# Weight parts laid out by use, three preparation buffers and a rewritten order in a fused convolution and SwiGLU kernel

## The chip, the cores and the metric

The kernel runs on one core of one Trainium2 chip. The metric is the device time of one execution in microseconds (us), as a median of several runs. Engines are named as in the profile: PE is TensorE's matmuls and PEld its weight loads, DVE is VectorE, ACT is ScalarE, POOL is GpSimd, SP is SyncE, which here issues almost all DMAs.

## What is computed

The input x has 8 sequences of 4096 tokens with 192 features. A causal convolution with 7 taps per head (8 heads of 24 features, taps through a softmax) is followed by a feed-forward block: RMS norm, a gate and a value product of 192 to 1536, SiLU, and an output product back to 192. All of it is in fp32.

```python
def _attn_ref(x, weight):
    w = np.exp(weight - np.max(weight, axis=-1, keepdims=True))
    w = w / (np.sum(w, axis=-1, keepdims=True) + 1e-09)
    ...
    out = np.einsum('hk,bskhg->bshg', w, x_unf)

def _moe_ref(x, w_gate, w_val, w_out, rms_g):
    rms = np.sqrt(np.mean(x * x, axis=-1, keepdims=True) + 1e-06)
    xn = x / rms * rms_g
    g = xn @ w_gate
    silu = g * (1.0 / (1.0 + np.exp(-g)))
    val = xn @ w_val
    return (silu * val @ w_out).astype(np.float32)
```

## The kernel before

**Tiles and pairs.** Tokens are taken in 32 pairs of 1024 (`PAIRS`), each two halves of 512. The first pair is computed with plain fp32 products (`plain`, `outer`). The second pair's gate and value products are plain too (line 871), while its output product already uses seven products instead of eight per block. From the third pair on all is in Strassen-Winograd form: sums of token halves (`x_sum`, line 827, words x1 to x4) meet sums of weight blocks, and each fp32 operand is split into three parts of the matmul format fp32r: a rounded high part (word n, line 667 or 669), a low part (word l, line 813) and a remainder (word d, line 815), in `split`. There are five token operands 0 to 4; operands 0, 1 and 2 are the tokens as they were fetched, 3 and 4 are the sums.

**Weight preparation.** During the second pair's products the ten weight operands (`NW`) are prepared, each by `prepare(o)` in six steps: an optional difference on POOL (line 749), the high part on DVE (752) with a scaled copy on ACT (756), the low part on DVE (758), a difference on POOL (762), the last part on ACT (764) and a store to DRAM (768). The parts lie in one of two buffers (`o % 2`) in the tile `part1`. The 1536 hidden features are six column blocks j; `FORM` says which of them use operands 2, 4, 6 and 8 (blocks 1, 2, 4, 5) and which use operand 9 (blocks 0 and 3). `blocks(o)` gives a slice of blocks to prepare: for the four blocks 1, 2, 4, 5, which are not evenly spaced, it gives all six.

**The ring.** The stored parts come back through `ring_load` (line 785) into ten slots, in the order in which TensorE uses them; a slot is loaded again when its last use is done. The first ten loads are issued by `ring_start`. The ring's tile takes the place of `lent`, in which the third pair's tokens lie (`tokens(2)`), so it can be loaded only when these have been read.

**Order.** Nothing is scheduled: every engine executes its instructions in the order written down in four tables. `LINE` holds the 110 words of TensorE for a pair: 68 product words of six matmuls (such as P1.1 or Q4.1: product name and block; A, B and E words belong to the blocks of form 0), and 42 output words (o1.0: output product 1, block 0). `ORDER` holds the words of the other engines for one pair, each with its engine ahead (V for DVE, A for ACT, G for POOL, S for SP); `p3` means that TensorE's line goes on by three words, and a trailing `+` or `-` that the word belongs to the next or the previous pair. `FIRST` is the same for the second pair, where `W` is the next step of the weight preparation and `R` is `ring_start`. `PLAIN` is the order of the second pair's 24 product cells: for each block the four cells a, b, c, d, of two halves each.

The other words: `ga` to `gd` is the SiLU of a cell on ACT (line 976), `ma` to `md` the product with the value half on DVE (line 983), which frees the cell's PSUM buffer (there are four); `f1`, `f3` copies and `f4`, `f5` sums (line 970) that complete cells in PSUM; `h1` to `h4` the sums of hidden blocks for the output products (line 953); `c1`, `s7`, `c2`, C22, C21 copies and sums of output accumulators, T11 to T22 the transposes of the output (line 941). For the pairs to come: `cv0` to `cv6` the taps (cv0 on ACT, line 433, the others on DVE, line 437), `sq`, `red`, `pow`, `bc`, `mul` the norm, `pl` the store of the normed tokens to a DRAM scratch, `ft` their fetch back in transposed form (line 638), `ld` the load of x (line 146), `st` the store of the output.

The second pair therefore ends so: its 24 cells, then its 42 output words, among which stand the third pair's sums and splits, in `ORDER`'s first rows; `R` stands at the end of `FIRST`, but takes effect when the last of these splits has read the tokens.

Of the kernel before, what the change touches and what calls it, by code (L numbers as in the profile page):

```python
# [20 lines left out]
def kernel(  # L21
# [11 lines left out]
    P = nc.NUM_PARTITIONS  # L33
# [24 lines left out]
    PAIRS = B * NB  # L58
# [13 lines left out]
    PLAIN = tuple((j, c) for j in range(NP) for c in "abcd")  # L72
    ORDER = (
# [28 lines left out]
    )  # L102
    LINE = (
# [615 lines left out]
    def blocks(o):  # L719

        kind = {2: 1, 4: 1, 6: 1, 8: 1, 9: 0}.get(o)
        mine = [j for j in range(NP) if kind in (None, FORM[j])]
        step = {b - a for a, b in zip(mine, mine[1:])}
        if len(step) > 1:
            return slice(0, NP)
# [557 lines left out]
```

## Time and profile before

| | us |
|---|---|
| median of 3 runs (2518.46 to 2523.32) | 2521.33 |
| the profiled execution | 2519.95 |
| its span, first to last instruction | 2518.1 |
| mean granted TensorE clock | 0.996 of full speed |

Of the rows below, those of a group read: line, engine, operation, tile written and tiles read, shape, count, then busy time, mean ns of one, and the engine's idle time ahead of them with what ended it. Rows of a timeline read: start, length, engine, line, operation; in brackets the engine's idle time just before and what ended it. Rows of windows read: from and to, length, busy us and count of PE, PEld, DVE, ACT and POOL, granted clock, busy share of the DMA engines, GB/s.

### The profile page before, as it was taken

What the parts mean: (1) busy time and instruction counts of PE and PEld (TensorE: products, weight loads), DVE (VectorE), ACT (ScalarE), POOL (GpSimd) and SP (SyncE); (2) the same over time, 40 slices, a digit from 0 to 9 for tenths busy, and PEclk for the clock granted to TensorE, in tenths of its full rate; (3) what the DMA queues carried; (4) which work ended last, traced back from release to release, by engine and by line L of the source; (5) the groups of instructions that cost most, each with busy time, mean ns of one, the idle gap of its engine ahead of it and who ended that gap; (6) DMA issues with size and microseconds to landing.
All of it is one profiled execution on the core that took longest, in us unless ns stands there. A gap on an engine that the chain in (4) does not pass through costs nothing.

```text
span 2518.1 us, 69213 instructions
## 1 busy us (share of the span) xinstructions
PE 2479.5 (98%) x29152; PEld 1919.2 (76%) x29152; DVE 2102.1 (83%) x2642; ACT 999.8 (40%) x1405; POOL 653.5 (26%) x538
## 2 busy tenths in 40 slices
PE   8988999999999999999999999999999999999998
PEld 5535777877777777878777778777777887777776
DVE  8676888898888898888898888898888898888874
ACT  6342443333443433443433443433443433443432
POOL 0551323122322122322122322122322122222222
PEclk9998999999999999999999999999999999999999
DMA  7272776666776666776666776666876666766653
GB/s 149 59 222 65 194 201 179 162 173 168 196 201 176 165 170 166 201 200 174 162 171 167 206 194 179 160 169 171 206 190 179 161 168 175 206 187 178 162 153 100
DMA packets 717415, 432.12 MB, mean 172 GB/s; under 512 B 510330, under 2 KB 703410, under 8 KB 717106
## 3 DMA queue, kind: packets, MB, share of 16 engines
q1 hardware_dynamic: 713360, 426.78, 65.0%
q8 instruction: 230, 3.77, 0.6%
q10 hardware_dynamic: 3746, 0.92, 0.2%
q14 instruction: 79, 0.65, 0.1%
HBM read 366.96 MB, written 60.56 MB: 170 GB/s over the span
## 4 chain that ended last, share of the span: by engine, by line
PE 92%; DVE 2%; DMA 1%; SPq 1%; issue 1%; POOL 1%; ACT 1%; DVEq 0%; POOLq 0%; ACTq 0%
PE ps L899 57%; PE ps L926 34%; PE ps L871 1%; DMA wd<-part 1%; SPq L230 0%; SPq L146 0%; POOL part L762 0%; DVE y L437 0%; DVE ht L1098 0%; DMA hs<-in_moe_w_out_dram 0%; DVE part L758 0%; DVE part L815 0%; DVE part L813 0%; DMA x<-in_x_dram 0%; DMA ht<-in_moe_w_gate_dram 0%
## 5 line engine op out<-in xcount | busy, mean ns | idle before, releaser
L899 PE MATMUL ps<-part,ring 64*128 64x512 f32 x12240 | 1447.6, 392 | 4.2
L899 PEld LDWEIGHTS ps<-part,ring 64*128 64x128 f32 x12240 | 1174.2, 184 | 264.2 <-issue 34.7
L976 ACT ACTIVATE tt<-ps 128x512 f32<-128x512 f32 x744 | 442.1, 599 | 1017.8 <-PE ps L899 939.4
L983 DVE TENSOR_TENSOR ht<-ps,tt 128x512 f32<-128x512 f32 x744 | 500.2, 686 | 211.6 <-ACT tt L976 204.3
L926 PE MATMUL ps<-ht,wo_sb 128*32 128x384 f32 (+2 forms) x7272 | 458.2, 380 | 12.8 <-DVE ht L953 12.0
L953 POOL TENSOR_TENSOR ht<-ht 128x512 f32<-128x512 f32 x152 | 209.2, 1386 | 898.9 <-PE ps L926 565.3
L926 PE MATMUL ps<-ht,x 128*32 128x384 f32 (+2 forms) x6696 | 419.5, 379 | 0.0
L926 PEld LDWEIGHTS ps<-ht,wo_sb 128*32 128x32 f32 x7272 | 322.9, 110 | 122.7 <-issue 23.3
L437 DVE SCALAR_TENSOR_TENSOR y<-xh,tp,y 128x1536 f32<-128x1536 f32 x186 | 349.2, 1877 | 13.7 <-ACT y L433 12.5
L926 PEld LDWEIGHTS ps<-ht,x 128*32 128x32 f32 x6696 | 294.8, 110 | 86.3
L970 DVE TENSOR_TENSOR ps<-ps,tt 128x1024 f32<-128x1024 f32 x240 | 295.6, 1232 | 57.7 <-PE ps L899 29.5
L667 ACT COPY tt<-ps 128x1024 f32<-128x1024 f32 (+1 forms) x152 | 121.6, 800 | 151.3 <-PE ps L926 148.9
L466 POOL TENSOR_SCALAR r<-r 128x8 f32<-128x8 f32 x31 | 6.1, 198 | 662.6 <-DVE r L461 662.5
L953 POOL TENSOR_TENSOR hs<-ht 128x512 f32<-128x512 f32 x120 | 153.9, 1294 | 64.9 <-DVE ht L983 64.9
L667 ACT COPY ps<-ps 128x1024 f32<-128x1024 f32 (+1 forms) x151 | 134.0, 887 | 85.3 <-DVE ht L983 40.1
L953 DVE TENSOR_TENSOR ht<-ht 128x512 f32<-128x512 f32 x220 | 167.1, 760 | 0.1
L926 PE MATMUL ps<-hs,x 128*32 128x384 f32 (+2 forms) x2232 | 149.3, 379 | 0.0
L926 PEld LDWEIGHTS ps<-hs,x 128*32 128x32 f32 x2232 | 100.5, 110 | 32.2
L813 DVE TENSOR_TENSOR part<-xb,part 128x1024 fp32r<-128x1024 f32 x87 | 105.9, 1217 | 0.0
L953 POOL TENSOR_TENSOR ht<-hs,ht 128x512 f32<-128x512 f32 x62 | 80.6, 1300 | 93.9 <-DVE ht L953 62.9
L433 ACT ACTIVATE y<-xh,tp 128x1536 f32<-128x1536 f32 x29 | 45.8, 1579 | 145.9 <-DMA xh<-in_x_dram 106.4
L815 DVE SCALAR_TENSOR_TENSOR part<-part,xb 128x1024 fp32r<-128x1024 f32 x87 | 103.5, 1218 | 0.0
(129 smaller groups left out, 1413.5 us busy)
## 6 DMA issues: line engine op xcount, KB each, us to landing
ring<-wd SPq DMA_DIRECT2D x1440, 192.0 KB
xb<-xd SPq DMA_DIRECT2D x60, 512.0 KB
xd<-xh SPq DMA_DIRECT2D x240, 96.0 KB
xh<-in_x_dram SPq DMA_DIRECT2D x192, 105.0 KB
xb<-xd SPq DMA_DIRECT2D x60, 256.0 KB
out_dram<-o_sb SPq DMA_DIRECT2D x126, 96.0 KB
wd<-part SPq DMA_DIRECT2D x9, 1152.0 KB
out_dram<-o_sb SPq DMA_DIRECT2D x62, 128.0 KB
```

Source lines behind the costliest of these rows:

```text
L433: nc.scalar.mul(y, xk, w)
L437: nc.vector.scalar_tensor_tensor(out=y, in0=xk, scalar=w, in1=y, op0=ALU.mult, op1=ALU.add)
L667: nc.scalar.copy(out=dst, in_=src)
L813: e.tensor_tensor(out=split_of(g, 1).bitcast(F32R), in0=src, in1=high, op=ALU.subtract)
L815: nc.vector.scalar_tensor_tensor(out=split_of(g, 2).bitcast(F32R), in0=high, scalar=1.0 + SPLIT, in1=src, op0=ALU.mult, op1=ALU.subtract,)
L871: nc.tensor.matmul(out=self.both(j, c)[:, h, :], lhsT=wf[HALF[h], k, 2 * j + f, :], rhs=rb[HALF[h], k, g, :], start=(k == 0), stop=(k == K ...
L899: nc.tensor.matmul(out=self.both(j, c)[:, h, :], lhsT=left[HALF[h]], rhs=right[HALF[h]], start=(first and q == 0), stop=True, skip_group_c ...
L926: nc.tensor.matmul(out=self.acc(b)[i * Q : (i + 1) * Q, at : at + n], lhsT=left, rhs=cols, start=fresh, stop=True, skip_group_check=True, ...
L953: engine[eng].tensor_tensor(out=dst, in0=a, in1=b, op=op)
L970: nc.vector.tensor_tensor(out=self.both(j, c), in0=self.both(j, "b"), in1=s5, op=ALU.add)
L976: nc.scalar.activation(out=tt[:, t, :], in_=self.both(j, c)[:, 0, :], func=AF.Silu)
L983: nc.vector.tensor_tensor(out=self.hv(j, "abcd".index(c)), in0=self.both(j, c)[:, 1, :], in1=tt[:, t, :], op=ALU.mult,)
```

## The change

- `HOME` gives every block a place: blocks of form 1 get places 0 to 3, those of form 0 places 4 and 5. The gate and value columns, the output rows and the stored parts are addressed through it, so `blocks(o)` is now always a dense slice: four blocks for operands 2, 4, 6, 8, two for operand 9, six for the others.
- `prepare` has three buffers instead of two (`o % 3`), and its work tiles move up behind them.
- `PLAIN` is a table of words and may hold output words among the cells (`products`); the row given holds the 24 cells in the same order as before, and no output word.
- `ORDER`, `FIRST` and `LINE` are new. In `FIRST` the third pair's sums and the splits of its operands 0, 1 and 2 now stand among the second pair's last cells, ahead of `R`; `run` remembers which of these were done (`ahead_done`) and leaves them out in `ORDER`'s first round. In `ORDER` the round begins earlier in the pair: 38 of TensorE's words instead of 33 belong to the previous pair.
- Some words change engine: n.1 from ACT to DVE, l.0, l.4 and x3 from DVE to POOL, f3.2 and f3.4 from ACT to DVE and f3.5 from DVE to ACT, and POOL has ten h sums instead of eleven.

```diff
+    HOME = tuple(
+        sum(FORM[:j]) if on else sum(FORM) + j - sum(FORM[:j]) for j, on in enumerate(FORM)
+    )
-    PLAIN = tuple((j, c) for j in range(NP) for c in "abcd")
+    PLAIN = (
+        "a0 b0 c0 d0 a1 b1 c1 d1 a2 b2 c2 d2 a3 b3 c3 d3 a4 b4 c4 d4 a5 b5 c5 d5",
+    )
     ORDER = (
-        "Ac1- An.3 p13- An.2 As7- An.4 Vd.3 Ac2- Acv0+ p12- Gh4.2- Vh4.3- Vl.0 Vh4.4- Vl.2",
-        "Vd.2 Vd.0 Vl.3 Vl.1 Vl.4 Vd.4 Vd.1 VC22- Gh4.0- Vh4.1- VT11- Vcv1+ Vh4.5- p8- VC21-",
...
+        "Agc.5- An.0 Agd.5- Agb.5- Vmc.5- p3- Vmd.5- Vmb.5- Vh1.5- Vh2.3- Vx1 Vd.0 Vn.1 Vx2",
+        "Vh3.5- Vh2.5- Ac1- p14- Vx4 Vh2.4- An.3 An.2 An.4 p2- As7- Ac2- Gl.0 p9- Acv0+ Vd.1",
+        "Vh4.5- Vl.3 Vl.2 Vh4.0- Vd.4 Vl.1 Vh4.1- Vh4.2- Vd.2 Vh4.3- p3- Gh4.4- VC22- p7- p1",
+        "VT22- Vd.3 p2 VC21- VT11- Vcv1+ p2 Vcv2+ VT12- p5 Agc.0 Agd.0 Vmc.0 Vcv3+ Vcv4+",
+        "Vmd.0 p1 Aga.0 p2 Af1.1 Vma.0 VT21- Agb.3 p1 Vcv5+ Vmb.3 Af3.1 p4 Gl.4 Vf4.1 Aga.1",
...
     FIRST = (
...
-        "Sld.1++ p2 Agc.5 Vx3+ Vmc.5 p2 Agd.5 p1 An.1+ Vmd.5 p1 Vh2.0 Vx1+ Vh1.5 Sld.2++",
-        "An.0+ p1 Gh2.2 Vx2+ p1 Gh2.4 Sld.3++ Vh3.5 p1 Vh2.3 p2 Vh2.1 Vx4+ p1 Vh2.5 p1 R",
-        "Sld.4++ Sld.5++ Sld.6++ Sld.7++",
+        "Vmc.4 p1 W p1 Gx3+ p1 Agd.4 Vmd.4 p1 Vx1+ Vh1.4 p1 Vn.1+ Sld.0++ p1 Aga.5 Vh3.4",
+        "Vma.5 Vx2+ p1 Vx4+ p2 An.2+ p3 Vd.1+ p1 Vl.2+ Sld.1++ p2 Vl.1+ An.0+ Vd.0+ Gl.0+ p1",
+        "Vh2.0 Vd.2+ p1 Vh2.1 p1 Vh2.2 R Sld.2++ Sld.3++ Sld.4++ Sld.5++ Sld.6++ Sld.7++",
     )
     LINE = (
-        "Ad.0 Bd.0 Ed.0 Aa.0 Ab.3 Ea.0 Ac.0 Ec.0 Bc.0 Bb.3 Ba.0 Eb.3 P1.1 Ab.0 P5.1 Eb.0 P6.1",
-        "Bb.0 Q1.1 P2.1 P7.1 Q2.1 P3.1 Aa.3 Q4.1 Ea.3 Ba.3 P4.1 P1.2 Q3.1 P5.2 P6.2 P2.2 Q1.2",
...
+        "Ac.0 Bc.0 Ec.0 P1.1 Ad.0 Aa.0 Bd.0 Ea.0 Ed.0 Ba.0 Ab.3 Bb.3 Eb.3 P5.1 P6.1 P2.1 Q1.1",
+        "Ab.0 Eb.0 Bb.0 Aa.3 P7.1 Q2.1 Ba.3 Ea.3 P3.1 Q4.1 Q3.1 P4.1 P1.2 Ac.3 P5.2 Ec.3 P6.2",
+        "P2.2 Q1.2 P7.2 P3.2 Bc.3 Q2.2 Q4.2 Q3.2 P4.2 P5.4 P1.4 Ad.3 Ed.3 P6.4 Bd.3 Q1.4 P2.4",
+        "P7.4 Q2.4 P3.4 P1.5 Q4.4 Q3.4 P4.4 P2.5 Q1.5 P5.5 P6.5 o1.0 o1.1 o1.3 o1.2 P7.5 P3.5",
+        "Q2.5 P4.5 Q4.5 Q3.5 o1.4 o1.5 o7.0 o7.1 o7.3 o7.2 o2.0 o6.1 o2.2 o2.3 o2.5 o6.2 o2.1",
...
     def blocks(o):
 
         kind = {2: 1, 4: 1, 6: 1, 8: 1, 9: 0}.get(o)
-        mine = [j for j in range(NP) if kind in (None, FORM[j])]
-        step = {b - a for a, b in zip(mine, mine[1:])}
-        if len(step) > 1:
-            return slice(0, NP)
-        return slice(mine[0], mine[-1] + 1, step.pop() if step else 1)
+        mine = sorted(HOME[j] for j in range(NP) if kind in (None, FORM[j]))
+        return slice(mine[0], mine[-1] + 1)
 
     def prepare(o):
...
-        st = room1[:, o % 2 * 3 * n : (o % 2 + 1) * 3 * n]
+        st = room1[:, o % 3 * 3 * n : (o % 3 + 1) * 3 * n]
...
-            room1[:, (6 + i) * n : (7 + i) * n].rearrange("p (j n) -> p j n", j=NP)
+            room1[:, (9 + i) * n : (10 + i) * n].rearrange("p (j n) -> p j n", j=NP)
...
-        r = (j * NW + o) * P
+        r = (HOME[j] * NW + o) * P
...
-                for j, c in PLAIN:
+                first = [w for row in PLAIN for w in row.split()]
+                for w in first:
+                    if w[0] == "o":
+                        self.step(int(w[1]), int(w[3]))
+                        yield
+                        continue
+                    j, c = int(w[1]), w[0]
...
-                                out=self.both(j, c)[:, h, :], lhsT=wf[HALF[h], k, 2 * j + f, :],
+                                out=self.both(j, c)[:, h, :], lhsT=wf[HALF[h], k, 2 * HOME[j] + f, :],
...
-            right = RIGHT[form][:, k]
+            right = RIGHT[form][:, HOME[k]]
...
+    ahead_done = set()
+
...
-                    if own_acts[act] <= p < PAIRS:
+                    if own_acts[act] <= p < PAIRS and (name, p) not in ahead_done:
                         ahead(eng, name, p)
+                        if w == 1:
+                            ahead_done.add((name, p))
```

More of the change, by code (lines that the diff above doesn't have):

```diff
@@ L876, in products @@
                         yield
-                todo = [w for w in line_of if w[0][0] == "o"]
+                todo = [w for w in line_of if w[0][0] == "o" and ".".join(w) not in first]
             else:
```

43 rows, old and new, of tables (FIRST, LINE, ORDER) are left out of this document.

## The prediction

> **What bounds the kernel now.** I read the page first, then the share of each engine by stage, then the timeline of the one stage in which TensorE stands still.
>
> ```profile
> span 2518.1 us, 69213 instructions
> PE 2479.5 (98%) x29152; PEld 1919.2 (76%) x29152; DVE 2102.1 (83%) x2642; ACT 999.8 (40%) x1405; POOL 653.5 (26%) x538
> ```
> TensorE is busy 98% of the span: only its idle time and its slow words can be won back. By stage (length, then each engine's busy time, granted clock, share of the DMA engines, GB/s):
>
> ```profile
> 124.76:195.62 70.86, 63.71 (x290) 28.21 (x289) 50.37 (x62) 28.24 (x44) 31.54 (x19) 1.00 0.65 201
> 195.62:222.50 26.88, 26.86 (x494) 20.45 (x492) 22.90 (x26) 6.84 (x9) 6.47 (x4) 1.00 0.15 45
> 222.50:234.44 11.94, 0.00 (x0) 0.00 (x0) 2.47 (x3) 1.57 (x1) 0.00 (x0) 0.69 0.50 107
> 235.88:313.87 77.99, 77.90 (x916) 62.28 (x912) 65.08 (x81) 30.25 (x41) 19.54 (x16) 0.97 0.67 174
> 313.87:2510.80 2196.93, 2192.82 (x26450) 1735.99 (x26448) 1863.12 (x2295) 867.75 (x1181) 562.01 (x459) 1.00 0.68 177
> 234.44:240.70 6.26, 6.25 (x34) 4.41 (x36) 6.22 (x7) 0.57 (x1) 0.00 (x0) 0.50 0.00 0
> ```
> The first row is the second pair's gate and value products: 70.86 us, 63.71 of them busy. The second is its output steps, without a hole. The third is the hole: 11.94 us without a matmul. Then comes the third pair, 77.99 us, and the last 29 pairs take 2196.93/29 = 75.76 us each, of which TensorE idles 4.1/29 = 0.14. After the hole the clock is granted at 0.5 for 6.26 us of work, which explains the third pair's 77.99 - 75.76 = 2.2 us; the hole's own mean of 0.69 puts the fall at 0.38 of it, 4.5 us after its start. The hole in the timeline:
>
> ```profile
> 217.27 5.72 SPq L785 DMA_DIRECT2D ring<-wd  x10
> 223.03 4.41 SPq L146 DMA_DIRECT2D xh<-in_x_dram  x4
> 230.36 1.57 ACT L433 ACTIVATE y<-xh,tp 128x1536 f32<-128x1536 f32 x1 [19.70 <-DMA xh<-in_x_dram]
> 231.97 1.82 DVE L437 SCALAR_TENSOR_TENSOR y<-xh,tp,y 128x1536 f32<-128x1536 f32 x1 [12.52 <-ACT y L433]
> 233.71 0.68 DVE L953 TENSOR_TENSOR ht<-ht 128x512 f32<-128x512 f32 x1
> 234.44 1.51 PE L926 MATMUL ps<-ht,wo_sb 128*32 128x384 f32 x12 [11.97 <-DVE ht L953]
> ```
> The ring's ten loads leave SP at 217.27, when the last split has read the tokens that lie in the ring's place. Behind them come the x loads of the fourth pair, ACT's first tap waits for these until 230.36, VectorE's second tap (L437) for ACT, and in VectorE's queue the sum (L953) that TensorE's last output step needs stands behind that tap. So SP's order and VectorE's order made the hole, not missing throughput.
>
> In the first stage TensorE waits for VectorE:
>
> ```profile
> PE ps L871 <- DVE ht L983: 7.2, 6, 2.2
> DVE part L752 <- DMA wd<-part: 5.3, 5, 2.0
> 172.63 0.56 DVE L752 TENSOR_SCALAR part<-part 128x768 uint32<-128x768 uint32 x1 [1.00 <-DMA wd<-part]
> 174.17 0.68 DVE L983 TENSOR_TENSOR ht<-ps,tt 128x512 f32<-128x512 f32 x1
> 174.91 2.85 PE L871 MATMUL ps<-xb,part 64*128 64x512 f32 x12 [0.38 <-DVE ht L983]
> 179.97 15.72 PE L871 MATMUL ps<-xb,part 64*128 64x512 f32 x72 [2.22 <-DVE ht L983]
> ```
> The weight preparation (L752) waits for the DMA that empties its buffer; the value product (L983) that frees a PSUM buffer stands behind it, and TensorE starts 0.06 us after that. The last six cells run without such a wait, 15.72/6 = 2.62 us each, so all 24 need 62.9 us instead of 70.86: 8.0 us lie there.
>
> **The change part by part.** Durations:
>
> ```profile
> L976 ACT ACTIVATE tt<-ps 128x512 f32<-128x512 f32 x744 | 442.1, 599 | 1017.8 <-PE ps L899 939.4 <-PE ps L871 38.9 <-DVE ht L953 29.4
> L983 DVE TENSOR_TENSOR ht<-ps,tt 128x512 f32<-128x512 f32 x744 | 500.2, 686 | 211.6 <-ACT tt L976 204.3
> L970 DVE TENSOR_TENSOR ps<-ps,tt 128x1024 f32<-128x1024 f32 x240 | 295.6, 1232 | 57.7 <-PE ps L899 29.5 <-ACT tt L667 18.6
> L815 DVE SCALAR_TENSOR_TENSOR part<-part,xb 128x1024 fp32r<-128x1024 f32 x87 | 103.5, 1218 | 0.0
> L667 ACT CAST part<-xb 128x1024 fp32r<-128x1024 f32 x87 | 88.0, 1045 | 34.1 <-DMA xb<-xd 31.7 <-DMA out_dram<-o_sb 2.4
> L669 DVE COPY tt<-ps 128x1024 f32<-128x1024 f32 x30 | 36.7, 1224 | 20.7 <-PE ps L899 20.7
> L953 POOL TENSOR_TENSOR ht<-ht 128x512 f32<-128x512 f32 x152 | 209.2, 1386 | 898.9 <-PE ps L926 565.3 <-DVE hs L953 331.2
> L762 POOL TENSOR_TENSOR part<-part 128x768 f32<-128x768 f32 (+1 forms) x10 | 18.2, 1823 | 35.1 <-DVE part L758 35.1
> L487 POOL TENSOR_TENSOR xh<-y,s 128x1536 f32<-128x1536 f32 x30 | 90.7, 3025 | 12.1 <-ACT ps L667 7.5 <-DMA ring<-wd 3.3 <-DVE s L479 1.2
> ```
> *Weight layout.* Operands 2, 4, 6 and 8 are prepared for four blocks instead of six, on 512 elements instead of 768. On GpSimd that takes four L762 from 1.82 to 1.39 or less (the 512-wide L953 row) and four L749 in proportion, some 3 us of its 31.54; VectorE and ACT save less. That the weights' columns are permuted (HOME) adds no instruction and takes none. *Three buffers.* L752 then waits for a store issued three preparations ago, not two: most of the 5.3 us of DMA waits goes. VectorE has 50.37 us of work in this stage; the splits that move in add one rounding, three remainders and low parts and two sums, 0.75 + 3 x 1.13 + 2 x 0.60 = 5.4, and 56 still fit in 62.9. What can stay are the hand-overs of a preparation between VectorE, ACT and GpSimd. I take the full 8.0; the other bound, with half the waits left, is 4.
>
> *The third pair's splits.* They move ahead of pair two's output steps, so the ring can be loaded once the remainders behind the last cell are done, and in the new order the second tap stands behind all h sums. SP issues the ring's ten loads (5.72) ahead of six x loads instead of four (4.41/4 = 1.1 each); both leave over 10 us earlier than today, and the fourth pair's first tap now stands in ACT's queue behind the copies of the output sums, so it finds its data. The hole (11.9) goes, and with it the slow clock: 2.2 in the third pair and 1.44 - 0.65 = 0.8 in the last output step.
>
> *What it costs.* The rounding of operand 1, now on VectorE, overwrites the preparation's buffers and so waits for the last stores to land: 2.0 us at the longest, if it is like the waits above. Behind it stands a value product that TensorE needs at its first output step, some 4 us later, so it is covered; beyond 4 us it would cost what is over. The split of operand 0 writes where the weights lay, so ACT can round it (1.05, L667) only when the last cell is done. Behind it on VectorE stand two remainders (L815; 1.13 each: two take 2.35 together in the timeline below, one 1.22), three h sums (0.60 each: 1.29 for two, less 0.69) and only then the value product (0.69) that frees the buffer for the seventh output step. GpSimd's low part, 1024 elements, is no row: between 1.39 x 2 = 2.8 (L953) and 3.03 x 2/3 = 2.0 (L487), I take 2.4 from the nearest, L762 x 4/3. If it excludes VectorE, the buffer comes 0.3 + 1.05 + 4.1 + 2.4 + 0.7 = 8.5 us after the last cell; six output steps cover 6 x 25.49/39 = 3.9. New stall: 4.6, or 2.2 if GpSimd runs beside. I take 4. Queued behind the rounding on ACT are the silus of the last three cells, behind the remainders their products, and behind TensorE's seventh step the other 35.
>
> That VectorE and GpSimd exclude each other in sums of two SBUF operands is seen in the steady stretch:
>
> ```profile
> 1048.78 1.29 DVE L953 TENSOR_TENSOR ht<-hs,ht 128x512 f32<-128x512 f32 x2
> 1057.19 2.35 DVE L815 SCALAR_TENSOR_TENSOR part<-part,xb 128x1024 fp32r<-128x1024 f32 x2
> 1065.26 2.97 POOL L953 TENSOR_TENSOR ht<-ht 128x512 f32<-128x512 f32 x2 [18.30 <-PE ps L926]
> 1067.58 2.27 DVE L437 SCALAR_TENSOR_TENSOR y<-xh,tp,y 128x1536 f32<-128x1536 f32 x1
> 1070.83 1.80 DVE L437 SCALAR_TENSOR_TENSOR y<-xh,tp,y 128x1536 f32<-128x1536 f32 x1
> ```
> The tap that starts while GpSimd is at work takes 2.27 instead of 1.80 and ends 1.6 us after GpSimd's two sums (1068.23). The Trainium skill ("SBUF — State Buffer", section "SBUF: two separate sides") says that the port pair of the two is an exclusive lock that a VectorE instruction with two SBUF inputs takes as well; it speaks against the change, which gives GpSimd more of them, and the trace agrees (2.27 against 1.80).
>
> *The annealed order, 29 times.* In each pair two low parts (2.4 each) and the sum x3 (1.4) go to GpSimd, one h sum comes back; VectorE gives up 2 x 1.13 and 0.6, takes one h sum (0.6), one f3 copy (1.22, L669) and one rounding. That rounding from SBUF is no row; 0.56 x 4/3 = 0.75 by L752, 1.22 by L669; I take 0.75. VectorE's sum is about unchanged. Two places decide.
>
> ```profile
> 999.96:1004.04 4.08, 4.08 (x38) 3.61 (x36) 4.08 (x6) 1.06 (x2) 0.00 (x0) 1.00 0.34 105
> 995.75:1039.40 43.65, 43.50 (x374) 37.01 (x372) 34.80 (x44) 20.02 (x28) 11.75 (x11) 1.00 0.68 197
> 1046.04:1071.53 25.49, 25.49 (x470) 19.33 (x469) 24.67 (x31) 8.53 (x11) 3.88 (x3) 1.00 0.59 128
> 1010.96:1011.64 0.68, 0.68 (x9) 0.68 (x7) 0.58 (x2) 0.68 (x1) 0.00 (x0) 1.00 0.79 242
> 1011.64:1012.66 1.02, 0.89 (x10) 0.50 (x7) 1.02 (x2) 0.18 (x1) 0.00 (x0) 1.00 0.58 202
> ```
> First the products: six unhindered words take 4.08 us, so 62 need 42.2, and 43.65 are used: 1.5 us go in waits. A word costs 0.68 unhindered (fourth row) and 1.02 where the next waits for a sum step (fifth). That chain is silu 0.60, product 0.69, sum 1.23 and some 0.5 of hand-overs, 3.0 us; with four words of lead (2.7) it stalls 0.3, plus 0.1 of restart. In the new line it stands so at Q4.2 and Q4.4, a shorter one at P7.2 and P4.5: together 1.4. Even, then: 0 +/- 0.3.
>
> Second the output steps. From the last product on, VectorE must pass two value products, 13 sums of 0.60, seven splits of 1.13 and the rounding before the last h sum: 1.3 + 7.8 + 7.9 + 0.75 = 17.8, and up to 1.3 while GpSimd's low part holds it up, 19.1. The output step that needs what follows comes 31 steps later, 31 x 0.654 = 20.3. It just fits; further on the last transposes of the pair are due about 0.5 us before the next pair's sixth word takes their buffer. I take 0 a pair, between -0.3 and +0.4.
>
> **Sum.** 8.0 + 11.9 + 0.8 + 2.2 - 4 + 0 = 18.9 us less than the profiled execution: span 2518.1 to 2499.2, its time 2519.95 to 2501.1. The median of the runs, 2521.33, is 1.4 above that execution, so **2502 us** in its terms.
>
> **Rivals.** (a) *The second pair pays more*: half its preparation waits stay (+4), and the new stall lets the clock fall, which costs about 3 more (0.8 + 2.2 above). For it: the hole's clock fell 4.5 us after its start; against it: the stage before kept 1.00 with a wait of 2.22 before 179.97. 2509. The Trainium skill ("TensorE: Matmul & The Clock Gate", section "What's actually happening") puts the fall at one idle window of about 3.4 us, free-running, which a stall of 4 us may or may not fill; by it the clock would fall in perhaps every second execution.
>
> (b) *The steady pairs get faster* by 0.3 each, since words with long lead (Q4.1) no longer stall: 29 x 0.3 = 9 less, 2493. For it: the 1.5 us that are there; against: as many short leads in the new line.
>
> (c) *The lock*, slower. GpSimd's second low part stands where VectorE ends the output steps. If GpSimd takes the ports first there, the split behind it, C21, two taps (1.75 each) and the transposes come 1.2 us later, 0.7 beyond their slack, and 0.4 more with 2.8 per low part: 1.1 a pair, 32 us against the 19 won: 2534. It decides from 0.65 us a pair on. For it: 2.27 against 1.80; against: by the sums above VectorE asks first, since GpSimd still holds an h sum.
>
> (d) *It doesn't do what it says*: the row of the second pair's products names cells alone and no output step, so no first outputs stand among them. That part of the change moves nothing; the time stays as forecast. The tail behind the last pair is the same in both.
>
> **How the numbers follow.** Forecast 0.60, (a) 0.15, (b) 0.13, (c) 0.12. The forecast's own bounds: second pair with hole and clock -21 (a stall of 2.2) to -11 (case (a), the stall 4.6), steady -9 to +12: from 2491 to 2522, whose far ends seldom meet. With (a) and (b) inside, 2491 to 2517 leaves out (c) and the upper end. A measurement of this kernel can tell 0.2%, 5 us. Faster: the first three, 0.88, less the top of the forecast's range, 0.02, plus 0.01 of (c): 0.87. Same 0.05, slower 0.08, from (c).
>
> **What would show it.** The hole before the third pair gone and the granted clock 1.00 there; the second pair's 24 cells in 63 us; a new wait of 2 to 5 us at its seventh output step, ended by a value product; the third pair at 75.8. The forecast is wrong if the pair's period differs from 75.76 by over 0.4, with VectorE's taps or GpSimd's low part ending the waits at the first words of a pair.

## The result, and the profile after

| | before | after |
| --- | --- | --- |
| median of the runs, us | 2521.42 (2518.46 to 2523.32) | 2490.49 (2490.08 to 2490.66) |
| profiled execution: time, span | 2519.95, 2518.1 | 2490.40, 2488.6 |

The ratio is 0.9878, with a 95% interval of 0.9861 to 0.9895: 31 us faster. The forecast was 2502, its range 2491 to 2517; the time lies half a microsecond under the range.

The engines' busy times on the page of the changed kernel:

```profile
PE 2469.0 (99%) x29152; PEld 1894.4 (76%) x29152; DVE 2112.0 (85%) x2645; ACT 949.5 (38%) x1345; POOL 839.6 (34%) x595
```

The same stages as before: the second pair's cells, its output steps in three pieces (six steps, a wait, the other 36), the third pair, the last 29 pairs.

```profile
125.03:187.03 62.00, 62.00 (x290) 27.80 (x288) 52.74 (x66) 26.60 (x43) 28.27 (x20) 1.00 0.64 201
187.03:191.20 4.17, 4.11 (x74) 3.07 (x72) 2.97 (x2) 2.52 (x4) 2.93 (x1) 1.00 0.00 0
191.20:195.27 4.07, 0.00 (x1) 0.03 (x1) 4.07 (x6) 0.00 (x0) 0.48 (x1) 0.96 0.19 61
195.27:220.29 25.02, 25.02 (x434) 18.74 (x434) 15.09 (x22) 4.91 (x6) 4.60 (x2) 0.94 0.46 97
220.29:295.66 75.37, 75.36 (x915) 59.36 (x914) 65.74 (x81) 28.61 (x39) 26.45 (x18) 1.00 0.68 180
295.66:2481.35 2185.69, 2185.18 (x26450) 1712.76 (x26448) 1875.31 (x2298) 821.60 (x1124) 743.02 (x514) 1.00 0.67 177
```

Set beside the rows of before, stage by stage:

| stage | before | after | difference | predicted |
| --- | --- | --- | --- | --- |
| second pair's cells | 70.86 | 62.00 | -8.86 | -8.0 |
| its output steps with the hole | 40.26 | 33.26 | -7.0 | -8.7 (-11.9 - 0.8 + 4) |
| third pair | 77.99 | 75.37 | -2.6 | -2.2 |
| last 29 pairs | 2196.93 | 2185.69 | -11.2 | 0 |
| all before and behind | 132.06 | 132.28 | +0.2 | 0 |

40.26 is the time from 195.62 to 235.88. The sum is 29.5, as the spans have it. Without the last 29 pairs it is 18.3, where the forecast had 18.9: everything that the prediction worked out at the start of the program came within 2 us, and what it took as zero, 29 times, made the difference. The pair went from 75.76 to 75.37.

The new stall is where it was foretold. The timeline of the changed kernel around the end of the cells; the rows of weight loads, of DMA issues and of TensorE up to the wait are left out:

```profile
187.15 1.04 ACT L671 CAST part<-ring 128x1024 fp32r<-128x1024 f32 x1 [6.07 <-PE ps L878]
188.10 1.57 ACT L983 ACTIVATE tt<-ps 128x512 f32<-128x512 f32 x3
188.23 1.23 DVE L816 SCALAR_TENSOR_TENSOR part<-part,ring 128x1024 fp32r<-128x1024 f32 x1 [1.53 <-ACT part L671]
188.27 3.40 POOL L814 TENSOR_TENSOR part<-ring,part 128x1024 fp32r<-128x1024 f32 x1 [12.01 <-ACT part L671]
189.37 2.86 DVE L960 TENSOR_TENSOR ht<-hs,ht 128x512 f32<-128x512 f32 x1
192.15 1.21 DVE L816 SCALAR_TENSOR_TENSOR part<-part,ring 128x1024 fp32r<-128x1024 f32 x1
193.28 1.28 DVE L960 TENSOR_TENSOR ht<-hs,ht 128x512 f32<-128x512 f32 x2
194.49 1.87 DVE L990 TENSOR_TENSOR ht<-ps,tt 128x512 f32<-128x512 f32 x3
...
195.27 1.51 PE L933 MATMUL ps<-ht,x 128*32 128x384 f32 x12 [4.13 <-issue]
```

ScalarE rounds operand 0 when the last cell is done (187.15) and only then runs the silus of the last three cells. On VectorE the remainder (L816) comes first, then an h sum (L960) that takes 2.86 instead of 0.69, since GpSimd's low part (L814) runs from 188.27 to 191.67; then another remainder, two sums, and at 194.49 the products (L990). The first of these frees the buffer, and TensorE's seventh output step starts at 195.27, after 4.13 us.

The steady pair is shorter in its product words: the first 372 matmuls of a pair take 43.22 instead of 43.65, against 42.16 if none of the 62 words waited (0.68 each). Three words of that stretch, Q4.2, P1.5 and Q4.4, in the pair that starts at 973.92:

```profile
973.92:1017.14 43.22, 43.20 (x374) 35.07 (x372) 36.49 (x44) 19.41 (x28) 14.02 (x12) 1.00 0.66 189
1001.73:1002.48 0.75, 0.75 (x8) 0.70 (x8) 0.00 (x0) 0.54 (x1) 0.00 (x0) 1.00 0.90 307
1011.43:1012.12 0.69, 0.69 (x8) 0.39 (x4) 0.64 (x1) 0.48 (x1) 0.69 (x1) 1.00 0.67 169
1012.12:1012.93 0.81, 0.81 (x9) 0.67 (x8) 0.66 (x1) 0.12 (x1) 0.81 (x2) 1.00 0.36 76
```

The prediction gave Q4.2 and Q4.4 a wait of 0.3 and a restart of 0.1 each, the wait being seen as a longer word ahead of the one that waits. Here the words ahead are not longer (P1.5 takes 0.69), and Q4.2 and Q4.4 lose 0.07 and 0.13.

The gain lies at two other words. First two rows of the changed kernel, the eight words from Aa.3 to Q3.1, with Q4.1 among them, and Q1.2 with P7.2; then Q2.2 with Q3.2 in the kernel before:

```profile
987.65:993.09 5.44, 5.44 (x50) 4.50 (x48) 5.27 (x7) 3.71 (x5) 1.30 (x2) 1.00 0.79 245
998.02:999.68 1.66, 1.65 (x14) 1.05 (x12) 0.95 (x2) 0.60 (x1) 0.79 (x1) 1.00 0.62 193
...
1021.67:1023.38 1.71, 1.69 (x16) 1.14 (x14) 1.01 (x2) 0.60 (x1) 0.06 (x1) 1.00 0.83 207
```

The eight words take 0.68 each: the 0.4 that Q4.1 cost in the kernel before is gone. So is the 0.3 of Q3.2, since Q2.2 and Q3.2 take 0.68 and 0.69 in the changed kernel. What came new is the 0.3 at P7.2.

### The profile page after: what moved, and what is told of

Its sections match the earlier page's. It is cut to its first block, busy times and chain, and to the rows that moved or that the text cites. A ratio compares the mean times of both kernels' runs of the same rounds, so it can differ in the third digit from the quotient of the medians.

```text
span 2488.6 us, 69159 instructions
## 1 busy us (share of the span) xinstructions
PE 2469.0 (99%) x29152; PEld 1894.4 (76%) x29152; DVE 2112.0 (85%) x2645; ACT 949.5 (38%) x1345; POOL 839.6 (34%) x595
## 4 chain that ended last, share of the span: by engine, by line
PE 95%; DVE 2%; DMA 1%; SPq 1%; issue 1%; POOL 1%; ACT 0%; DVEq 0%; POOLq 0%; ACTq 0%
PE ps L906 58%; PE ps L933 34%; PE ps L878 2%; DMA ht<-in_moe_w_gate_dram 0%; SPq L234 0%; DVE ht L1105 0%; SPq L150 0%; DVE y L441 0%; DMA x<-in_x_dram 0%; DVE ht L960 0%; DMA hs<-in_moe_w_out_dram 0%; DVE part L341 0%; POOL part L332 0%; DVE part L326 0%; DVE part L816 0%
## 5 line engine op out<-in xcount | busy, mean ns | idle before, releaser
L906 PEld LDWEIGHTS ps<-part,ring 64*128 64x128 f32 x12240 | 1147.3, 184 | 276.8 <-DVE ps L977 32.6
L983 ACT ACTIVATE tt<-ps 128x512 f32<-128x512 f32 x744 | 440.1, 599 | 932.0 <-PE ps L906 882.2
L990 DVE TENSOR_TENSOR ht<-ps,tt 128x512 f32<-128x512 f32 x744 | 492.0, 686 | 156.7 <-ACT tt L983 145.8
L960 POOL TENSOR_TENSOR hs<-ht 128x512 f32<-128x512 f32 x150 | 204.2, 1369 | 829.2 <-DVE ht L990 829.2
L977 DVE TENSOR_TENSOR ps<-ps,tt 128x1024 f32<-128x1024 f32 x240 | 295.2, 1230 | 103.8 <-PE ps L906 84.9
L960 POOL TENSOR_TENSOR ht<-ht 128x512 f32<-128x512 f32 x121 | 156.5, 1294 | 540.8 <-PE ps L933 302.9
L960 DVE TENSOR_TENSOR ht<-ht 128x512 f32<-128x512 f32 x251 | 170.3, 690 | 5.9 <-PE ps L933 5.8
L960 DVE TENSOR_TENSOR ht<-hs,ht 128x512 f32<-128x512 f32 x156 | 128.9, 844 | 3.2
L671 ACT COPY tt<-ps 128x384 f32<-128x384 f32 (+1 forms) x122 | 90.8, 744 | 103.1 <-PE ps L933 98.2
L933 PE MATMUL ps<-hs,x 128*32 128x128 f32 (+2 forms) x2232 | 130.0, 379 | 0.0
L671 ACT CAST part<-tt 128x1024 fp32r<-128x1024 f32 x60 | 62.8, 1048 | 124.2 <-DVE tt L828 122.5
L816 DVE SCALAR_TENSOR_TENSOR part<-part,xb 128x1024 fp32r<-128x1024 f32 x87 | 105.9, 1217 | 0.0
L814 POOL TENSOR_TENSOR part<-tt,part 128x1024 fp32r<-128x1024 f32 x30 | 101.2, 3373 | 0.0
```

The source lines that it names most:

```text
L671: nc.scalar.copy(out=dst, in_=src)
L814: e.tensor_tensor(out=split_of(g, 1).bitcast(F32R), in0=src, in1=high, op=ALU.subtract)
L816: nc.vector.scalar_tensor_tensor(out=split_of(g, 2).bitcast(F32R), in0=high, scalar=1.0 + SPLIT, in1=src, op0=ALU.mult, op1=ALU.subtract,)
L906: nc.tensor.matmul(out=self.both(j, c)[:, h, :], lhsT=left[HALF[h]], rhs=right[HALF[h]], start=(first and q == 0), stop=True, skip_group_c ...
L933: nc.tensor.matmul(out=self.acc(b)[i * Q : (i + 1) * Q, at : at + n], lhsT=left, rhs=cols, start=fresh, stop=True, skip_group_check=True, ...
L960: engine[eng].tensor_tensor(out=dst, in0=a, in1=b, op=op)
```

## The experiments

Times are medians; the kernel before took 2521.8 to 2522.5 beside them. A pair's length is the stretch of the last 29 pairs over 29, as in the windows shown.

### What a pair's words wait for

**The buffer a sum writes.** Q4 accumulates into cell d, which VectorE's sum f5 fills; f5 stands behind a value product (L990; L983 in the kernel before) that gives back a PSUM buffer. VectorE's rows in the changed kernel, first the product and f5.2 (L977), then the product and f5.4:

```profile
999.53 0.69 DVE L990 TENSOR_TENSOR ht<-ps,tt 128x512 f32<-128x512 f32 x1 [0.71 <-ACT tt L983]
1000.33 1.23 DVE L977 TENSOR_TENSOR ps<-ps,tt 128x1024 f32<-128x1024 f32 x1
...
1010.24 0.69 DVE L990 TENSOR_TENSOR ht<-ps,tt 128x512 f32<-128x512 f32 x1 [0.68 <-ACT tt L983]
1010.85 1.22 DVE L977 TENSOR_TENSOR ps<-ps,tt 128x1024 f32<-128x1024 f32 x1
```

The first sum starts 0.11 us after the product's end (999.53 + 0.69 = 1000.22), the second 0.08 before it (1010.93). Their queues are alike; the buffers are not. f5.2 writes the buffer that the product has just read and given back, f5.4 the one of cell d.3, given back earlier. So f5.2 has to wait for the completion of the product just ahead of it on its own engine, and f5.4, by the waits in the built program, only for that of the instruction before. In the kernel before f5.1 writes the product's own buffer, and starts 0.10 after it:

```profile
1010.48 0.69 DVE L983 TENSOR_TENSOR ht<-ps,tt 128x512 f32<-128x512 f32 x1 [0.69 <-ACT tt L976]
1011.27 1.23 DVE L970 TENSOR_TENSOR ps<-ps,tt 128x1024 f32<-128x1024 f32 x1
```

One run gives f5.4 the product's own buffer, another gives f5.1 of the kernel before a different one.

```
same_bank   (changed kernel, open)
-  i = next(i for i in pool4 if i in full4) if full else (used + pool4)[0]
+  whole_ones = [i for i in pool4 if i in full4]
+  i = whole_ones[-1 if name == (4, "d") else 0] if full else (used + pool4)[0]

other_bank  (kernel before, open, behind the line that chooses i)
+  if name == (3, "a") and self.p > 1 and len(pool4) > 1:
+      i = pool4[-1]
```

> The changed kernel, but the sum f5.4 of every pair takes the PSUM buffer that the product of cell a.4, just ahead of it on VectorE, has freed, and the word P1.5 takes that of cell d.3 (the two swap places; no instruction is moved or added). In the trace of the changed kernel a sum that writes the buffer its own engine has just read starts 0.11 us after the product's end (f5.2, f5.1), one that writes another buffer 0.08 before it (f5.4). Theory B (that 0.19 us is why Q4.4 with four words of lead loses only 0.12 and not the 0.38 of the prediction): Q4.4 starts 0.2 to 0.3 us late, pair 75.37 to 75.55 - 75.70, time 2496 to 2500. Theory N (the buffer does not matter, the chain is 2.7 us long in any case): pair 75.37 +/- 0.05, time 2490 to 2492.

> The kernel before, but from the third pair on the word Aa.3 takes the PSUM buffer freed last (cell a.1's) and the sum f5.1, which comes behind it, that of cell b.0, freed earlier; no instruction is moved. Theory B (a sum that writes the buffer its engine has just read starts 0.19 us later, and that wait sets Q4.1): the 0.29 + 0.09 us at Q4.1 fall to 0.1 to 0.15, pair 75.76 to 75.5, time 7 us less: 2514 to 2516. Theory N (the four-word lead is short with either buffer): Q4.1 as before, 2521 to 2523.

With the same buffer 2499.60 (2498.56 to 2500.08), 9.1 more than the changed kernel. Its last 29 pairs, P1.5, and VectorE's product and sum:

```profile
296.51:2490.67 2194.16, 2189.39 (x26449) 1737.89 (x26448) 1878.91 (x2298) 822.70 (x1124) 740.26 (x514) 1.00 0.68 177
1014.75:1015.74 0.99, 0.87 (x9) 0.45 (x5) 0.98 (x2) 0.60 (x1) 0.99 (x2) 1.00 0.61 148
...
1013.56 0.69 DVE L991 TENSOR_TENSOR ht<-ps,tt 128x512 f32<-128x512 f32 x1 [0.69 <-ACT tt L984]
1014.36 1.23 DVE L978 TENSOR_TENSOR ps<-ps,tt 128x1024 f32<-128x1024 f32 x1
```

The sum now starts 0.11 after the product's end (1014.25), the word ahead of Q4.4 takes 0.99 instead of 0.69, and the pair 2194.16/29 = 75.66 instead of 75.37. The converse in the kernel before: 2513.48, ratio 0.9966 (0.9953 to 0.9979). Its last 29 pairs, and the word ahead of Q4.1:

```profile
314.46:2503.85 2189.39, 2189.13 (x26450) 1705.36 (x26448) 1860.37 (x2295) 867.99 (x1181) 561.41 (x459) 1.00 0.68 177
1009.95:1010.63 0.68, 0.68 (x8) 0.38 (x5) 0.68 (x2) 0.14 (x1) 0.00 (x0) 1.00 0.87 273
...
1008.75 0.69 DVE L985 TENSOR_TENSOR ht<-ps,tt 128x512 f32<-128x512 f32 x1 [0.67 <-ACT tt L978]
1009.35 1.22 DVE L972 TENSOR_TENSOR ps<-ps,tt 128x1024 f32<-128x1024 f32 x1
```

The sum starts 0.09 before the product's end (1009.44), Aa.3 takes 0.68 instead of 0.97 on the mean of the pairs, and the pair 75.50 instead of 75.76. Theory B holds both ways: no instruction moved, and a quarter of a microsecond a pair came or went. The buffer moves the sum by 0.19 us. Another 0.1 is TensorE's: Q4.4 starts 0.05 after the sum's end in the changed kernel (1012.07 and 1012.12), and 0.15 after it in same_bank (1015.59 and 1015.74). Its weight loads in the one and the other:

```profile
1012.12 1.00 PEld L906 LDWEIGHTS ps<-part,ring 64*128 64x128 f32 x10 [0.27 <-DVE ps L977]
...
1015.71 0.79 PEld L907 LDWEIGHTS ps<-part,ring 64*128 64x128 f32 x8 [0.52 <-ACT tt L984]
```

The load has waited in both. In the changed kernel it waits for the sum alone, the matmuls of P1.5 run on meanwhile, and only the restart is lost. In same_bank it waits for the sum and, one wait behind the other, for ScalarE's silu (L984), which has read the same buffer. That this second wait is what makes 0.15 of 0.05 is argued and not tried by itself; but to have waited long isn't enough, since P7.5 in copies_back (below) starts 0.05 after its sum with 0.88 us of idle time ahead of it.

**Waits that share a chain.** In the changed kernel P7.2 waits for the sum f4.2 (0.18, and 0.12 at its restart).

```
p7_later    (changed kernel, LINE)
-  P2.2 Q1.2 P7.2 P3.2 Bc.3 Q2.2 Q4.2 ...
+  P2.2 Q1.2 Bc.3 P7.2 P3.2 Q2.2 Q4.2 ...
```

> The changed kernel with the word P7.2 one place later (Q1.2 Bc.3 P7.2 P3.2 Q2.2 Q4.2), so that it no longer waits for f4.2 (0.18 + 0.12 us in every pair). Q4.2 keeps its four words behind the silu's cell. If waits on one chain share their time (shared): the wait ahead of P7.2 had given Q4.2's chain its time; it turns up at Q4.2, pair 75.25 to 75.45, time 2487 to 2493. If each short lead pays on its own, as the prediction added them up (apart): 0.30 less a pair, 75.06, time 2482.

2491.37 (2490.97 to 2491.78). The last 29 pairs, and the word Q2.2 ahead of Q4.2:

```profile
295.85:2481.68 2185.83, 2182.09 (x26450) 1721.30 (x26448) 1878.50 (x2298) 821.44 (x1124) 747.27 (x514) 1.00 0.68 177
1001.20:1002.16 0.96, 0.84 (x8) 0.40 (x5) 0.81 (x1) 0.08 (x1) 0.00 (x0) 1.00 0.97 160
```

P7.2's wait is gone and Q2.2 takes 0.96: the 0.28 have moved to Q4.2, and with its restart (0.78 in place of 0.68) the 0.38 are those of Q4.1 in the kernel before. The pair stays at 75.37. So the price that the prediction gave Q4.2 is right for the place; in the changed kernel only 0.07 of it is paid, since TensorE has already stood at P7.2 while the chain for Q4.2 ran.

**A word moved in the kernel before.** The first edit gives Q4.1 a fifth word of lead; the second also puts c.1 ahead of d.1 and of the reduction.

```
q4_later    (kernel before, LINE)     q4_c_first  (the same, and ORDER)
-  ... Aa.3 Q4.1 Ea.3 Ba.3 ...        -  Vf5.1 Vred+ p3 Agd.1 Agc.1 p1 Aga.3 Vmd.1 Vmc.1 ...
+  ... Aa.3 Ea.3 Q4.1 Ba.3 ...        +  Vf5.1 p2 Agc.1 p1 Agd.1 Vmc.1 Vred+ p1 Aga.3 Vmd.1 ...
```

> The kernel before with one edit: in each pair the word Q4.1 stands one word later (Aa.3 Ea.3 Q4.1 Ba.3), so it has five words of lead instead of four behind the sum it waits for. Nothing moves between engines. Theory W (the steady pair's length above 74.3 us is set by waits of single words, whatever engine does what): the 0.29 us wait ahead of Q4.1 and most of the 0.09 us of its restart go, pair 75.76 to about 75.4, time 29 x 0.35 = 10 us less: 2511. Theory E (the pair got shorter because low parts and x3 left VectorE): nothing here relieves VectorE, so the wait only turns up at another word; time 2521 +/- 2.

> The kernel before with Q4.1 one word later, as in q4_later, and cell c.1's gate and product ahead of d.1's and ahead of the 2.2 us of the reduction, so that the next word P1.2, which took the wait over (0.26 + 0.12), gets its buffer from c.1 instead. No work changes engines. Theory O (the order of words and queue alone holds the 0.4 us): the wait goes at last, pair 75.66 to 75.3 - 75.45, time 2510 to 2514. Theory V (VectorE's queue is full there, so whatever is put first another word waits): pair 75.6 to 75.9, time 2518 to 2525.

The first took 2520.69, the second 2518.83 (ratios 0.9993 and 0.9985). Both missed what I hoped for (theories W and O): the pair is 75.72 and 75.66. The first one's wait turns up ahead of P1.2, where P4.1 takes 0.94; P1.2 wants the buffer that the product of Q4.1's cell frees. In the second it turns up two words later, where Q3.1 takes 0.90. Where VectorE's queue is full, moving a word moves the wait; the exchange of buffers took 0.19 us out of the chain itself.

**The engines.** Two runs undo moves between engines in the changed kernel and leave its order.

```
low_dve      (ORDER and FIRST)  Gl.0 -> Vl.0, Gl.4 -> Vl.4, Gx3 -> Vx3
copies_back  (ORDER and FIRST)  Vn.1 -> An.1, Vf3.2 -> Af3.2, Vf3.4 -> Af3.4, Af3.5 -> Vf3.5
```

> The changed kernel with the low parts l.0 and l.4 and the sum x3 of every pair back on VectorE (GpSimd loses 2.6 + 3.4 + 1.4 us a pair, VectorE gains 2 x 1.2 + 0.7 = 3.1). Theory W: the waits of the product words stay as they are (1.07 us above 42.16) and VectorE's extra work is hidden in the output steps or pays back in lock waits; pair 75.36 +/- 0.15, time 2486 to 2494; the second pair's stall at its seventh output step gets 1 to 3 us shorter as the h sum no longer waits 2.2 us for GpSimd. Theory E: the gain of 0.40 a pair goes, 75.76 or more, time 2500 or more.

> The changed kernel with the rounding n.1 and the copies f3.2 and f3.4 back on ScalarE and f3.5 on VectorE, as in the kernel before. Theory W: the copies ended ahead of what waits for them on either engine (f3.2 ended 0.06 us before the product word that f4.2 also needs), so pair 75.36 +/- 0.1, time 2488 to 2493. Theory E: 0.1 to 0.4 a pair lost, time 2493 to 2502.

2521.57 and 2519.76: either one loses the whole gain of 31 us, or nearly so. The last 29 pairs take 2214.42/29 = 76.36 and 2213.51/29 = 76.33, a microsecond more than with the change. Where it goes in the first, on VectorE:

```profile
293.88:2508.30 2214.42, 2202.97 (x26450) 1714.52 (x26448) 1904.06 (x2383) 821.87 (x1124) 540.89 (x430) 1.00 0.67 175
994.72:995.91 1.19, 0.84 (x8) 0.38 (x4) 1.19 (x3) 0.24 (x1) 0.00 (x0) 1.00 0.52 128
...
992.91 1.22 DVE L814 TENSOR_TENSOR part<-tt,part 128x1024 fp32r<-128x1024 f32 x1
994.04 1.23 DVE L977 TENSOR_TENSOR ps<-ps,tt 128x1024 f32<-128x1024 f32 x1
995.18 0.68 DVE L990 TENSOR_TENSOR ht<-ps,tt 128x512 f32<-128x512 f32 x1
```

The low part l.4 (L814) pushes f4.1 and the product behind it 1.2 us back; that product frees the buffer of Aa.3, so the word ahead takes 1.19; P4.1 and P1.2, further on, lose another 0.3. The output steps, where l.0 and x3 came back, take 27.6 a pair in both kernels. In the second, f3.5 on VectorE (L673) holds up f4.5 (L977), and P7.5 waits 1.0 in every pair (the word ahead of it):

```profile
297.02:2510.53 2213.51, 2186.47 (x26450) 1716.63 (x26448) 1828.99 (x2241) 869.99 (x1181) 714.39 (x514) 1.00 0.67 175
1029.11:1030.84 1.73, 0.85 (x18) 0.39 (x11) 1.73 (x3) 0.00 (x0) 1.08 (x1) 1.00 0.89 304
...
1026.59 1.23 DVE L673 COPY tt<-ps 128x1024 f32<-128x1024 f32 x1 [0.70 <-PE ps L906]
...
1029.57 1.22 DVE L977 TENSOR_TENSOR ps<-ps,tt 128x1024 f32<-128x1024 f32 x1
```

All other words take what they take in the changed kernel, within 0.03 us on the mean of the pairs, so of the four words moved back f3.5 alone costs the microsecond.

My theory W, that the engines don't matter, falls; E, that relief on the sum of VectorE's work made the gain, isn't what these show either, since in copies_back VectorE does less (2063.4 busy in all, against 2112.0). What counts is which instruction stands ahead of which word. Q4.1 and Q3.2 take 0.68 and 0.69 in both runs, as in the changed kernel, so it is the new order that gave these two their time, and not the moves between engines; which part of the order was not tried.

### The second pair's cells

```
two_buffers   (changed kernel)  o % 3 -> o % 2, work tiles from 9 + i to 6 + i
six_blocks    (changed kernel, blocks)  + if kind == 1: return slice(0, NP)
three_before  (kernel before)   o % 2 -> o % 3, work tiles from 6 + i to 9 + i
```

> The changed kernel with two buffers for the weight parts instead of three. As the prediction put it (buffers): the store waits of the preparation come back and with them 4 to 8 of the 8.9 us that the second pair's cells won (62.00 to between 66 and 70), time 2494.5 to 2498.5. If the new order of that stage alone won them (order): 62 to 63, time 2490 to 2492. The steady pairs stay at 75.37 in both.

> The changed kernel with operands 2, 4, 6 and 8 prepared for all six blocks again (768 elements, not 512; the weights keep their places). As the prediction put it (hidden): some 3 us more on GpSimd and less on the others, behind the cells, which stay at 62 to 62.6; time 2490 to 2491.5. If the shorter preparation is what made the cells free of waits (short): 64 to 66, time 2492.5 to 2495.

> The kernel before with three buffers for the weight parts instead of two and nothing else. If the store waits made TensorE's waits in the second pair's cells, as the prediction put it (buffers): the cells take 63 to 66 instead of 70.87, and the hole behind them, which starts when the ring's place is free, moves with them: time 5 to 8 us less, 2514 to 2517. If the order of the preparation on VectorE and ScalarE makes them (order): 69 to 71, time 2520 to 2523.

2491.53, 2495.10 and 2517.75 (ratio to before 0.9986, 0.9977 to 0.9996). Cells and output steps of the first, and its store waits:

```profile
124.60:186.63 62.03, 62.03 (x290) 27.71 (x289) 48.56 (x64) 26.27 (x43) 27.30 (x20) 1.00 0.65 201
186.63:221.88 35.25, 30.02 (x506) 22.51 (x505) 24.43 (x31) 7.32 (x10) 7.98 (x3) 0.90 0.34 76
...
DVE part L753 <- DMA wd<-part: 8.5, 5, 2.6
```

The waits for stores are back, 8.5 us of them on VectorE, and the cells take 62.03 all the same: in the new order of that stage nothing that TensorE needs stands behind them. They come out later. VectorE's rounding of operand 1 waits for the last store until 182.40 instead of 180.07, all behind it is late, and TensorE's idle time at the seventh output step is 5.23 instead of 4.13. Those of the second:

```profile
125.00:189.48 64.48, 62.98 (x290) 27.44 (x288) 53.57 (x63) 28.09 (x43) 32.62 (x20) 1.00 0.68 217
189.48:225.11 35.63, 29.05 (x508) 21.74 (x506) 25.78 (x32) 7.32 (x10) 7.06 (x3) 0.90 0.34 75
```

Here the cells lose 2.5 and the rounding (L673) waits 3.3 for the last store, so the seventh step stands 6.58. Three buffers in the kernel before win 2.0 of the 8.9:

```profile
124.88:193.70 68.82, 63.36 (x291) 28.36 (x289) 54.06 (x62) 28.22 (x44) 31.84 (x19) 1.00 0.68 207
```

No store wait is left there, and TensorE still idles 5.5 us (68.82 - 63.36). So neither buffers nor shorter operands alone carry the 8.9: undone singly, they cost the cells 0 and 2.5. That the rest lies in the new order of that stage is concluded from this; the order was not tried by itself.

### The hole, and the new stall

```
x_first      (kernel before, FIRST)
-  ... Vh2.5 p1 R Sld.4++ Sld.5++ Sld.6++ Sld.7++
+  ... Vh2.5 p1 Sld.4++ Sld.5++ Sld.6++ Sld.7++ R
tap_behind   (kernel before, ORDER)
-  ... VT11- Vcv1+ Vh4.5- p8- ...
+  ... VT11- Vh4.5- Vcv1+ p8- ...
```

> The kernel before with the last four x loads of the fourth pair ahead of the ring's ten loads on SP. As the prediction put it (SP's order and VectorE's order together made the hole): ScalarE's first tap finds its data some 8 us earlier, the hole of 11.94 shrinks to under 3, the clock stays up, 10 to 14 us less: 2508 to 2512. If the ring's loads are what the third pair then waits for (ring): the hole moves to the first words of the third pair, under 4 us won: 2517 to 2522.

> The kernel before with VectorE's second tap behind the last h sum of the pair instead of ahead of it (one swap, all pairs). If VectorE's order alone made the hole (order): the output steps run through, and the third pair starts some 12 us earlier: 2507 to 2512. If the late tap only holds up what stands behind it on VectorE (the sums and transposes that free the buffers of the third pair's second and third word; buffers): TensorE stops there instead, 0 to 4 us won: 2517 to 2522. In the steady pairs nothing waits for that sum at once, +/- 0.1 a pair.

2508.32 (ratio 0.9943, 0.9928 to 0.9958) and 2522.80. The output steps of the first, then what follows those of the second (27.51):

```profile
195.55:223.03 27.48, 27.48 (x506) 20.84 (x504) 26.56 (x30) 8.32 (x10) 6.49 (x4) 1.00 0.17 50
...
222.94:234.07 11.13, 0.00 (x1) 0.01 (x2) 2.34 (x3) 1.58 (x1) 0.00 (x0) 0.67 0.48 96
```

With the x loads ahead of the ring's the hole is gone, clock and all. With the tap behind the last sum the output steps run through, and the same 11 us stand ahead of the third pair, where a sum of the output (L1000) behind the late tap holds its words up. SP's order made the hole; VectorE's order only said at which word it showed.

```
gates_first  (changed kernel, FIRST; the same words are left out of ORDER's round for pair two)
-  ... Vx4+ p2 An.2+ p3 Vd.1+ p1 Vl.2+ Sld.1++ p2 Vl.1+ An.0+ Vd.0+ Gl.0+ ...
+  ... Vx4+ p2 Agb.5 An.2+ Vmb.5 p3 Agc.5 Vd.1+ Vmc.5 p1 Vl.2+ Sld.1++ p2 Agd.5 Vl.1+ Vmd.5 An.0+ Vd.0+ Gl.0+ ...
gates_low    (as gates_first, FIRST)  Gl.0+ -> Vl.0+
```

> The changed kernel with the last three gates and products of the second pair (cells b, c, d of block 5) moved, in the second pair alone, ahead of the rounding and the split of operand 0. If the stall at the seventh output step (4.13 us of idle TensorE, and a slow clock behind it) comes from the product that frees its buffer standing behind that rounding, the two remainders and the h sum held up by GpSimd's low part (queue): the 42 output steps take 27.5 to 28.5 instead of 33.25, time 2485 +/- 1. If another step is late next, such as an h sum that still waits 2.2 us for GpSimd (next wait): 30 to 32, time 2488 to 2490.

> As the kernel before it, and the low part of operand 0 in that place on VectorE instead of GpSimd (only there; the steady pairs keep theirs). Queue: no further gain at the output steps, time within 0.5 of the other kernel. Next wait: 1 to 3 us less than the other kernel, since no h sum waits for GpSimd's 3.4 us any more.

2484.68 (2484.26 to 2485.03; ratio to before 0.9849, 0.9835 to 0.9864) and 2484.98. The output steps of the first:

```profile
186.77:214.54 27.77, 27.65 (x507) 20.78 (x506) 21.86 (x27) 6.44 (x8) 8.03 (x3) 1.00 0.45 97
```

27.77 instead of 33.26: the stall was worth 5.5 us, 4.07 of idle time and 1.4 of the slower clock behind it. The queue theory holds. GpSimd's low part still delays an h sum there (2.86 us); with the low part on VectorE, in gates_low, that sum takes 0.69 again, but it wins nothing more. This kernel is faster than both, by 5.8 us than the changed one.

## Why the prediction was off

**The step that failed** is the one under "the annealed order, 29 times": "with four words of lead (2.7) it stalls 0.3, plus 0.1 of restart. In the new line it stands so at Q4.2 and Q4.4 [...]: together 1.4. Even, then: 0 +/- 0.3." It took one row, of Q4.1 in the kernel before, as the price of a lead of four words, and gave it to two other places. In neither is more than a part of it paid. At Q4.4 the sum writes another buffer than the product ahead of it, so its chain is 0.19 us shorter, TensorE starts 0.1 sooner behind it, and the four words cover all but the restart; same_bank brings the wait back, 0.29 a pair, and other_bank takes it from Q4.1 itself. At Q4.2 the wait at P7.2 covers it; p7_later uncovers it. Together the two lose 0.2 where I had 0.8. P7.2 loses 0.30; P4.5 isn't among these 62 words at all, since it stands behind the first output steps, and loses 0.12 in either kernel. The rest is lost in pieces of some 0.1 or less at words that I hadn't named (Ac.0, P6.2, P6.4, P6.5). So the words lose 1.06 and not 1.4, and the pair moved by 0.39, beyond my bound of 0.3. Rival (b), a pair 0.3 faster, is what came, and for the reason that it gave: Q4.1 no longer stalls, and Q3.2 doesn't either. It had a chance of 0.13; the argument against it, "as many short leads in the new line", counted leads in words and not what ran in them.

**The rest, in order.** *The cells* were sized nearly right, 8.86 for 8.0, but the reason was half wrong: the prediction took the store waits as the cause, and two_buffers shows them back without the cells being slower, and three_before without them is only 2.0 faster. So the size was in part luck. *The hole*: right in size; by x_first SP's order suffices, and VectorE's order, which the prediction named beside it, is by tap_behind no cause of the lost time. *The third pair*: -2.6 for -2.2, of which 0.4 is what every pair won. *The new stall*: right place, right chain, 4.13 for 4, which was a choice between 2.2 and 4.6. Mis-sized was the low part on GpSimd, 3.40 for 2.4; but it starts 0.04 behind VectorE's remainder and runs beside it for 1.2 us, so the sum came out near. The clock did fall, as in rival (a): 0.94 over the 25 us behind the stall, at 1.4 us, most of the 1.7 by which the output steps won less than forecast. That rival's rule from the Trainium skill ("TensorE: Matmul & The Clock Gate", section "What's actually happening"), an idle window of about 3.4 us, agrees with this one: 4.13 us of idle time were enough, and in the kernel before 2.22 were not. By that rule a stall of 4 us holds a whole free-running window in about one case of five ((4 - 3.4)/3.4, an estimate from that figure), and not in "every second execution". The two rows would fit any length between 2.22 and 4.13. The four runs of the changed kernel lie within 0.6 us of each other, less than the 1.4 that a fall costs, so the clock seems to have fallen in all of them; how often it does isn't settled.

*The engines' moves*, taken as even in VectorE's sum: the sum is even, 2102.1 to 2112.0, yet undoing either set costs a microsecond a pair. *Rival (c)*, the lock, didn't come although its premise did: the low part of operand 4, which ran towards the end of the output steps, takes

```profile
L814 POOL TENSOR_TENSOR part<-tt,part 128x1024 fp32r<-128x1024 f32 x30 | 101.2, 3373 | 0.0
```

3.37 us on average, more than the 2.8 of the upper bound, and still the output steps of a steady pair take 27.6 us on the mean, as in the kernel before; in low_dve, without it, they take the same time. *Rival (d)* was right that no output step stands among the cells, and changed no number.

## What to carry to other kernels

A wait that one row shows is the price of that place: before it is carried to another, follow its chain there, the buffer each instruction writes and the waits ahead of it that already give it time. Where an engine's queue is full next to the bound, moving a word moves the wait; look instead for time in the chain, such as a buffer that was freed earlier. A term that repeats 29 times deserves the closest working, since 0.4 us of it outweighed every error at the start.

## What the runs showed of the hardware

Two VectorE instructions overlap: the second starts 0.08 to 0.09 us before the first one's end. Where it has to wait for the first one's completion, here since it writes the PSUM buffer that the first has read, it starts 0.10 to 0.11 us after it. A TensorE word whose weight load has waited took 0.75 to 0.81 us in place of 0.68, even where the matmuls ahead ran on during the wait (Q4.4, 0.81). Q4.4 started 0.05 us after the end of the sum that it waited for, and 0.15 after it in same_bank, where a second wait stood beside the first. GpSimd's low part of 1024 elements took 2.4 to 3.4 us, and a VectorE sum beside it 2.86 in place of 0.69. VectorE's rounding of 1024 elements out of SBUF took 0.69 us, where ScalarE's took 1.04.
